# Where the high word of a weight decode is held while the main loop runs

## The chip, the cores and the metric

One core of a Trainium2 chip runs the whole program. The metric is the device time of one execution in microseconds (us), given as the median over runs. The kernel before takes 1439.48 us (three runs, 1436.52 to 1439.56).

## The reference, cut to what matters

The program computes an attention whose keys and values are first packed to 32 rows per head, then a gated layer, then a second layer with two products of x:

```python
p_packed = sm_attn(p, k, v)                 # 8 batches, 8 heads, 32 packed rows, 64 wide
x = sm_attn(q, p_packed, p_packed)          # 576 rows a batch -> 4608 x 512
h = x @ w_in                                # 512 x 2048
x = (h * sigmoid(h)) @ w_out                # 2048 x 512
a = x @ w1; b = x @ w2                      # 512 x 1024 each
out = ((a * b) @ w3) @ wo2                  # 1024 x 1024, 1024 x 512
```

The weights reach the chip as 64-bit words and have to be turned into 32-bit floats there. That is the work this change touches.

## The kernel before, in words

**Decode.** A weight tile of 128 x 512 is loaded as 64-bit words (`raw`). `Decode` (L167) makes floats of it in five instructions. ScalarE scales the high word (L179, shown in the profile under the helper's line L82) and shifts the low word. VectorE shifts the high word into place (L183, `z` or `zi`), and then joins the high word's sign with the low word (L185, written to `raw`). GpSimd adds the two (L189). The scaled high word goes either back into `raw` itself, which lies in SBUF, or into a PSUM tile `ps_dec`; the argument `ps` says which. A tile of w_out is then split into a high part on ScalarE and a low part on GpSimd (`wo<-z`, line L91).

**Which tiles.** `fill` (L701) holds the first 32 decodes in this order: eight tiles of w_in, w_out tiles 0 to 7, eight more of w_in, w_out tiles 8 to 15. A plan written by hand (`START`, L70) says where each is called (`F`) and loaded (`L`), beside the attention's own steps (`P0`, `S0`, ...), the products of packed rows and w_in (`T`, `D`) and stores (`W`). Whoever calls `acc_bank(1, ...)` (L158) gets one of two of the four PSUM banks that later hold the sums of the second product. `bank` (L163) gives one of two banks with the tag `f`, which scores (`ps_s`), transposes (`ps_t`), attention sums (`ps_o`), packed rows (`ps_pk`) and the products of w_in (`ps_m`) share.

**The main loop.** Each item is one batch, half and 128 columns of the hidden layer. `emit_h` makes `ps_h` with 6 matmuls; `emit_g` makes `sg` on ScalarE, `gg` on VectorE (L846), `gh` on ScalarE and `gl` on GpSimd; three items later `emit_x2` adds gh and gl times a w_out tile to four banks `ps_x` with 12 matmuls. There are 2 banks of `ps_h`, 4 buffers of `gg` and 4 each of `gh` and `gl`. So PE can run ahead with `ps_h`, but only by as many items as these buffers hold. Items 0 to 31 use w_out tiles 0 to 7, four rounds of them; items 32 to 39 are the first that use tiles 8 to 15. Between the items stand the packs (`Pack`, L359) of later batches, each with scores, a softmax and a transpose, from item 26 on.

**What sets the order.** The code is written item by item, and a scheduler then orders the instructions of every engine by a simulated time and hands out the buffers; each engine works through its own list strictly in order. `acc` is filled when `emit_x2` is first called, in item 3. From then on, `if acc` is true while the code is written.

Of the kernel before, what the change touches and what calls it, by code (L numbers as in the profile page):

```python
# [23 lines left out]
def attention_swiglu_chain(  # L24
# [133 lines left out]
    def acc_bank(y, name):  # L158

        turns[y] += 1  # L160
        return ps_acc.tile([128, 512], F32, tag=f"acc{2 * y + turns[y] % 2}", name=name)

    def bank(name):  # L163
        return ps_f.tile([128, 512], F32, tag="f", name=name)
# [76 lines left out]
    def at_room(n):  # L241
        return at.tile([128, 512], I32, tag="z", name="z", bufs=NZ)
# [14 lines left out]
    acc = {}  # L257
# [439 lines left out]
    def finish_fill(n, d):  # L697
# [8 lines left out]
            if kind == "i" else w_out[128 * i:128 * i + 128, :] for kind, i in order  # L706
        ],
        finish_fill, fill_raw, lambda n: zi[order[n][1]].bitcast(I32) if order[n][0] == "i" else at_room(n),
        lambda: None if acc else acc_bank(1, "ps_dec"),
    )  # L710


# [688 lines left out]
```

## Time and profile before

| what | value |
|---|---|
| median of three runs | 1439.48 us |
| the profiled execution's own time | 1437.96 us |
| its span | 1436.1 us |
| PE busy in the span | 1390.7 us (97%) |
| DVE, ACT, POOL busy | 901.6, 672.2, 605.5 us |

PE is TensorE, PEld its weight load, DVE VectorE, ACT ScalarE, POOL GpSimd. The average hides stages: PE is busy nearly everywhere, except in roughly the first 180 us, in which the 32 decodes run. So that stretch is looked at by itself.

### The profile page before, as it was taken

How to read it: one execution, taken by the hardware profiler on the slowest of the kernel's cores; microseconds unless marked ns; L12 is line 12 of the kernel's file. 1: busy time of each engine (PE TensorE's matmuls, PEld its weight loads, DVE VectorE, ACT ScalarE, POOL GpSimd, SP SyncE). 2: the span in 40 equal slices, each digit the busy share in tenths (PEclk: the TensorE clock that was granted, in tenths of full speed). 3: DMA queues.
4: the chain of work that ended last, by engine and by line, in shares of the span. 5: the costliest groups of instructions: out<-in, count | busy, mean ns of one | idle time of the engine just before them, and what ended most of it. 6: DMA issues, size and time to landing. Idle time of an engine off the chain costs nothing.

```text
span 1436.1 us, 25890 instructions
## 1 busy us (share of the span) xinstructions
PE 1390.7 (97%) x9548; PEld 1308.4 (91%) x9548; DVE 901.6 (63%) x1687; ACT 672.2 (47%) x1474; POOL 605.5 (42%) x626
## 2 busy tenths in 40 slices
PE   7799899999999999999999999999999999999998
PEld 5578899899999999999998998999999999999998
DVE  5897756558766488666578855635454553645453
ACT  6866556655666555664556544323232231322221
POOL 2778755856779657687567534100000000000000
PEclk9999899999999999999999999999999999999999
DMA  8697544844568343563557667011010110101000
GB/s 319 198 308 253 163 150 142 265 152 146 170 184 249 123 155 121 170 190 116 178 162 252 204 228 298 23 38 46 15 60 1 60 29 31 59 2 60 1 30 30
DMA packets 135967, 193.07 MB, mean 134 GB/s; under 512 B 14496, under 2 KB 92576, under 8 KB 135328
## 3 DMA queue, kind: packets, MB, share of 16 engines
q1 hardware_dynamic: 125344, 178.82, 39.1%
q10 hardware_dynamic: 10496, 12.59, 2.5%
q8 instruction: 75, 1.23, 0.4%
q14 instruction: 52, 0.43, 0.1%
HBM read 132.38 MB, written 58.98 MB: 133 GB/s over the span
## 4 chain that ended last, share of the span: by engine, by line
PE 70%; DVE 9%; DMA 7%; issue 4%; POOL 4%; ACT 4%; SPq 2%; ACTq 0%; DVEq 0%; POOLq 0%
PE ps_ab L1236 24%; PE ps_x L100 6%; PE ps_x L98 6%; PE ps_x L99 6%; PE ps_o L98 5%; PE ps_o L99 5%; PE ps_o L100 5%; PE ps_h L98 3%; PE ps_h L100 3%; PE ps_h L99 3%; SPq L115 2%; DMA mr<-m_d 1%; DMA m_d<-ms 1%; POOL z L189 1%; DVE sbd L251 1%
## 5 line engine op out<-in xcount | busy, mean ns | idle before, releaser
L98 PE MATMUL ps_x<-gh,wo 128*128 128x288 f32 x1024 | 301.9, 298 | 2.7 <-ACT gh L82 1.2
L99 PE MATMUL ps_x<-gh,wo 128*128 128x288 f32 x1024 | 301.0, 296 | 0.0
L100 PE MATMUL ps_x<-gl,wo 128*128 128x288 f32 x1024 | 289.1, 297 | 1.9 <-POOL gl L91 1.6
L91 POOL TENSOR_TENSOR gl<-gg,gh 128x288 fp32r<-128x288 f32 x256 | 227.9, 893 | 101.5 <-ACT gh L82 82.5
L1236 PE MATMUL ps_ab<-xct,w 128*128 128x256 f32 x1728 | 223.0, 284 | 1.7 <-DVE r L1257 1.4
L1236 PEld LDWEIGHTS ps_ab<-xct,w 128*128 128x128 f32 x1728 | 215.6, 190 | 3.0 <-DVE r L1257 1.6
L98 PEld LDWEIGHTS ps_x<-gh,wo 128*128 128x128 f32 x1024 | 193.0, 189 | 6.1 <-DVE xs L883 2.0
L99 PEld LDWEIGHTS ps_x<-gh,wo 128*128 128x128 f32 x1024 | 193.2, 189 | 2.1 <-issue 1.2
L100 PEld LDWEIGHTS ps_x<-gl,wo 128*128 128x128 f32 x1024 | 188.1, 189 | 4.3 <-POOL gl L91 3.6
L82 ACT ACTIVATE gh<-gg 128x288 fp32r<-128x288 f32 x256 | 112.8, 443 | 165.8 <-DVE gg L846 158.2
L91 POOL TENSOR_TENSOR mq<-mr,mq 128x256 fp32r<-128x256 f32 x168 | 136.7, 814 | 109.0 <-DVE mq L86 54.4
L846 DVE SCALAR_TENSOR_TENSOR gg<-sg,ps_h 128x288 f32<-128x288 f32 x256 | 114.6, 448 | 107.3 <-ACT sg L841 55.3
L1236 PE MATMUL ps_ab<-xcb,w 128*128 128x256 f32 x1296 | 177.5, 283 | 0.7 <-ACT w L82 0.4
L98 PE MATMUL ps_h<-a,mq 128*128 128x288 f32 x512 | 155.9, 305 | 18.0 <-DVE gg L846 13.8
L1236 PEld LDWEIGHTS ps_ab<-xcb,w 128*128 128x128 f32 x1296 | 168.1, 189 | 5.6 <-ACT w L82 0.6
L1257 DVE TENSOR_TENSOR r<-p,ps_ab 128x512 f32<-128x512 f32 x72 | 49.2, 683 | 184.3 <-PE ps_ab L1236 184.1
L99 PE MATMUL ps_h<-a,mq 128*128 128x288 f32 x512 | 152.4, 298 | 0.0
L100 PE MATMUL ps_h<-a,mq 128*128 128x288 f32 x512 | 151.9, 297 | 0.0
L841 ACT ACTIVATE sg<-ps_h 128x288 f32<-128x288 f32 x256 | 103.4, 404 | 82.3 <-PE ps_h L100 48.6
L98 PEld LDWEIGHTS ps_h<-a,mq 128*128 128x128 f32 x512 | 96.7, 189 | 25.9 <-DVE gg L846 19.0
L82 ACT ACTIVATE p<-ps_ab 128x512 f32<-128x512 f32 x72 | 43.1, 598 | 146.2 <-PE ps_ab L1236 139.8
L100 PE MATMUL ps_o<-w,abh 128*128 128x512 f32 x280 | 109.5, 391 | 0.0
(172 smaller groups left out, 2645.3 us busy)
## 6 DMA issues: line engine op xcount, KB each, us to landing
mr<-m_d SPq DMA_DIRECT2D x144, 128.0 KB, 2.6
raw<-in_moe_w_dram SPq DMA_DIRECT2D x32, 512.0 KB, 4.4
wz<-wi_d SPq DMA_DIRECT2D x48, 256.0 KB, 3.8
m_d<-ms SPq DMA_DIRECT2D x96, 128.0 KB, 3.0
x_d<-xs SPq DMA_DIRECT2D x20, 576.0 KB, 3.4
raw<-in_moe_w_out_dram SPq DMA_DIRECT2D x22, 512.0 KB, 4.3
out_dram<-ob SPq DMA_DIRECT2D x36, 256.0 KB, 2.0
vr<-in_v_dram SPq DMA_DIRECT2D x14, 640.0 KB, 4.1
```

The source lines that it names most:

```text
L82: A.activation(out=dst, in_=src, func=ACTF.Copy, scale=mul)
L91: (eng or V).tensor_tensor(out=lo, in0=src, in1=hi.bitcast(F32), op=ALU.subtract)
L98: T.matmul(out=dst, lhsT=wh, rhs=xh, start=start, stop=False)
L99: T.matmul(out=dst, lhsT=wl, rhs=xh, start=False, stop=False)
L100: return T.matmul(out=dst, lhsT=wh, rhs=xl, start=False, stop=stop)
L115: return eng.dma_start(out=out, in_=in_)
L189: G.tensor_tensor(out=z, in0=z, in1=word(I32, 0), op=ALU.add)
L251: (act_copy if plain else V.tensor_copy)(dst[r, 0, :, r], src[r])
L841: ins = A.activation(out=sg, in_=ps, func=ACTF.Tanh, scale=0.5)
L846: ins = V.scalar_tensor_tensor(out=gg, in0=sg, scalar=1.0, in1=ps, op0=ALU.add, op1=ALU.mult)
L1236: T.matmul(out=bank[:, x], lhsT=w[:, wp], rhs=xt[:, kt, xp], start=first and (x, kt, n) == (0, 0, 0), stop=last and (x, kt, n) == (1, 1, 2 ...
L1257: V.tensor_tensor(out=dst, in0=p, in1=q, op=op)
```

## The change

The condition stays, but its first branch now gives a shared bank where it gave nothing. The first 14 decodes, written before `acc` is filled, keep their banks. The other 18 (w_out tiles 6 and 7, w_in tiles 8 to 15, w_out tiles 8 to 15) write their high word to one of the two `f` banks and no longer into `raw`.

```diff
         finish_fill, fill_raw, lambda n: zi[order[n][1]].bitcast(I32) if order[n][0] == "i" else at_room(n),
-        lambda: None if acc else acc_bank(1, "ps_dec"),
+        lambda: bank("ps_dec") if acc else acc_bank(1, "ps_dec"),
     )
```

A bank is held from the write on ScalarE to the second read on VectorE, so the scheduler can place such a decode only where one of the two banks is free, between scores, transposes and products. That moves instructions on all engines. VectorE before, at the last decode (`z_2326` is made of w_out tile 15, `gg` are the items' activations, `mq` a prepared piece of packed w_in):

```order
L846 SCALAR_TENSOR_TENSOR gg_1631<-sg_1629,ps_h_1610 128x288
L86 CAST mq_174<-mr_1607 128x2x128
L883 TENSOR_SCALAR xs_1665<-ps_x2_1415 128x288
L846 SCALAR_TENSOR_TENSOR gg_1673<-sg_1671,ps_h_1646 128x288
L86 CAST mq_174<-mr_1643 128x2x128
L883 TENSOR_SCALAR xs_1665<-ps_x2_1417 128x288
L423 TENSOR_REDUCE mx_1699<-ps_s_1685 128x1
L183 TENSOR_SCALAR z_2326<-raw_2264 128x512
L185 SCALAR_TENSOR_TENSOR raw_2264<-raw_2264 128x512
L423 TENSOR_REDUCE mx_1699<-ps_s_1692 128x1
```

This decode stands behind 27 activations, beside the first pack's scores. VectorE now, from the transposes of the third pack (`e`) through the decodes of w_out tiles 13 and 14 (`z_2214`, `z_2271`):

```order
L91 TENSOR_TENSOR e_2195<-ps_t_2196,e_2194 128x384
L91 TENSOR_TENSOR e_2195<-ps_t_2200,e_2194 96x256
L846 SCALAR_TENSOR_TENSOR gg_2637<-sg_2635,ps_h_2616 128x288
L86 CAST mq_174<-mr_2613 128x2x128
L183 TENSOR_SCALAR z_2214<-ps_dec_2215 128x512
L185 SCALAR_TENSOR_TENSOR raw_2119<-ps_dec_2215,raw_2119 128x512
L846 SCALAR_TENSOR_TENSOR gg_2674<-sg_2672,ps_h_2648 128x288
L86 CAST mq_174<-mr_2645 128x2x128
L183 TENSOR_SCALAR z_2271<-ps_dec_2272 128x512
L185 SCALAR_TENSOR_TENSOR raw_2224<-ps_dec_2272,raw_2224 128x512
L469 STREAM_TRANSPOSE pkT_2327<-pk_2322 128x64
L846 SCALAR_TENSOR_TENSOR gg_2710<-sg_2708,ps_h_2685 128x288
```

These two stand behind 42 and 43 activations, and tile 15's behind 44. The first of the last eight decodes (tile 8) moves from behind 16 activations to behind 30.

GpSimd before, at w_out tiles 10 to 12 (`wo10`, `wo11`, `wo12` are the low parts):

```order
L189 TENSOR_TENSOR z_1966<-z_1966,raw_1869 128x512
L189 TENSOR_TENSOR z_2025<-z_2025,raw_1975 128x512
L91 TENSOR_TENSOR wo10_1972<-z_1966,wo10_1972 128x512
L91 TENSOR_TENSOR gl_1523<-gg_1520,gh_1522 128x288
L91 TENSOR_TENSOR wo11_2031<-z_2025,wo11_2031 128x512
L91 TENSOR_TENSOR gl_1565<-gg_1562,gh_1564 128x288
L225 MEMSET mbd_1905 128x1024
L189 TENSOR_TENSOR z_2095<-z_2095,raw_2034 128x512
L91 TENSOR_TENSOR gl_1602<-gg_1599,gh_1601 128x288
L189 TENSOR_TENSOR z_2199<-z_2199,raw_2104 128x512
L189 TENSOR_TENSOR z_2255<-z_2255,raw_2208 128x512
L91 TENSOR_TENSOR wo12_2101<-z_2095,wo12_2101 128x512
```

GpSimd now, at tiles 13 to 15 (`v` is a split of a pack's values, `wi` one of w_in for the packs' products):

```order
L91 TENSOR_TENSOR v_2340<-vr_2192,v_2339 128x768
L189 TENSOR_TENSOR z_2271<-z_2271,raw_2224 128x512
L91 TENSOR_TENSOR v_2340<-vr_2192,v_2339 96x512
L91 TENSOR_TENSOR wo13_2221<-z_2214,wo13_2221 128x512
L91 TENSOR_TENSOR mq_174<-mr_2682,mq_174 128x2x128
L91 TENSOR_TENSOR wo14_2278<-z_2271,wo14_2278 128x512
L189 TENSOR_TENSOR z_2343<-z_2343,raw_2281 128x512
L91 TENSOR_TENSOR wi_2782<-wz_2780,wi_2782 128x512
L91 TENSOR_TENSOR mq_174<-mr_2718,mq_174 128x2x128
L91 TENSOR_TENSOR wi_2787<-wz_2785,wi_2787 128x512
L91 TENSOR_TENSOR gl_2640<-gg_2637,gh_2639 128x288
L91 TENSOR_TENSOR wo15_2350<-z_2343,wo15_2350 128x512
```

The last w_out tiles no longer alternate with single `gl`; they stand between value splits, `mq` and `wi`, and between `wo10` and the end of `wo15` GpSimd now has 4 adds `z`, 5 low parts `wo`, 2 pairs of `v`, 5 `mq`, 5 `gl` and 2 `wi`. On PE, over the same stretch (from the product with tile 10's low part to that with tile 15's), stand 183 matmuls, among them the `ps_h` of items 39 to 47: PE's list now has `ps_h` of item 46 ahead of the low part of tile 13, whose product belongs to item 37.

## Rows read from the trace of the kernel before

**Rows 1.** Stretches of the decode phase: us, busy by engine, PEclk, DMA share, GB/s
```profile
60.00:80.00 20.00, 16.57 (x98) 13.78 (x98) 18.02 (x29) 12.93 (x28) 18.75 (x16) 1.00 0.98 322
80.00:100.00 20.00, 19.37 (x130) 17.61 (x129) 18.54 (x27) 15.34 (x32) 14.48 (x14) 1.00 0.95 301
100.00:120.00 20.00, 17.38 (x103) 13.82 (x103) 17.45 (x28) 11.01 (x27) 15.68 (x17) 1.00 0.93 302
120.00:140.00 20.00, 20.00 (x144) 19.04 (x144) 13.64 (x18) 15.15 (x32) 17.77 (x17) 1.00 0.79 255
140.00:160.00 20.00, 16.60 (x105) 15.05 (x105) 16.69 (x29) 12.33 (x30) 19.07 (x18) 0.91 0.67 203
160.00:180.00 20.00, 17.31 (x111) 17.08 (x110) 15.31 (x35) 10.05 (x29) 12.57 (x14) 0.83 0.39 113
180.00:200.00 20.00, 20.00 (x156) 20.00 (x155) 11.19 (x35) 10.30 (x26) 8.88 (x10) 1.00 0.41 133
200.00:240.00 40.00, 40.00 (x307) 39.82 (x306) 26.14 (x71) 21.92 (x53) 22.92 (x25) 1.00 0.41 131
```

**Rows 2.** Who PE waited for, 60 to 180 us: total, times, longest
```profile
PE ps_h L98 <- DVE gg L846: 9.8, 9, 3.3
PE ps_x L100 <- POOL gl L91: 1.6, 3, 1.2
```

**Rows 3.** VectorE's decode forms, 0 to 250 us: busy us, mean ns, idle before
```profile
L185 DVE SCALAR_TENSOR_TENSOR raw<-raw 128x512 int32<-128x512 int32 x18 | 21.2, 1175 | 0.0
L183 DVE TENSOR_SCALAR z<-raw 128x512 int32<-128x512 int32 x10 | 8.4, 840 | 4.9 <-ACT raw L82 4.9
L183 DVE TENSOR_SCALAR zi<-raw 128x512 int32<-128x512 int32 x8 | 8.1, 1018 | 0.1
L183 DVE TENSOR_SCALAR zi<-ps_dec 128x512 int32<-128x512 int32 x8 | 5.4, 681 | 4.8 <-ACT ps_dec L82 4.8
L185 DVE SCALAR_TENSOR_TENSOR raw<-ps_dec,raw 128x512 int32<-128x512 int32 x8 | 5.4, 680 | 0.0
```

**Rows 4.** Line L183 over the whole run: ns min/median/max, first and last
```profile
L183 DVE TENSOR_SCALAR z<-raw x30: 386/424/1474, 59.7 to 674.7; 128x512 int32<-128x512 int32 x30
L183 DVE TENSOR_SCALAR z<-ps_dec x26: 673/678/692, 42.4 to 820.3; 128x512 int32<-128x512 int32 x26
```

**Rows 5.** VectorE in order of time: the last decode, and the 44th activation
```profile
145.12 0.99 DVE L183 TENSOR_SCALAR z<-raw 128x512 int32<-128x512 int32 x1
...
201.90 0.46 DVE L846 SCALAR_TENSOR_TENSOR gg<-sg,ps_h 128x288 f32<-128x288 f32 x1
```

**Rows 6.** GpSimd's forms, 60 to 180 us: busy us, mean ns, idle before
```profile
L91 POOL TENSOR_TENSOR gl<-gg,gh 128x288 fp32r<-128x288 f32 x36 | 33.7, 944 | 8.0 <-ACT gh L82 7.7 <-POOL zi L189 0.2
L189 POOL TENSOR_TENSOR z<-z,raw 128x512 int32<-128x512 int32 x11 | 15.8, 1437 | 1.3 <-DVE raw L185 1.3
L91 POOL TENSOR_TENSOR wo<-z,wo 128x512 fp32r<-128x512 f32 x11 | 15.3, 1390 | 0.0
L91 POOL TENSOR_TENSOR mq<-mr,mq 128x256 fp32r<-128x256 f32 x16 | 12.9, 804 | 6.7 <-DVE mq L86 6.1 <-issue 0.3 <-DMA x_d<-xs 0.3
...
L91 POOL TENSOR_TENSOR wi<-wz,wi 128x512 fp32r<-128x512 f32 x3 | 3.9, 1323 | 0.0
L91 POOL TENSOR_TENSOR v<-vr,v 128x768 fp32r<-128x768 f32 x2 | 3.9, 1934 | 0.0
L91 POOL TENSOR_TENSOR v<-vr,v 96x512 fp32r<-96x512 f32 x2 | 2.5, 1272 | 0.0
```

**Rows 7.** VectorE in order of time: from a pack's transpose to the next pack's `e`
```profile
162.09 0.25 DVE L469 STREAM_TRANSPOSE pkT<-pk 128x64 f32<-128x64 f32 x1 [1.94 <-ACT pk L464]
...
179.75 0.88 DVE L91 TENSOR_TENSOR e<-ps_t,e 128x384 fp32r<-128x384 f32 x2 [0.37 <-ACT e L82]
```

**Rows 8.** Line L189, GpSimd's add, over the whole run: ns min/median/max
```profile
L189 POOL TENSOR_TENSOR z<-z,raw x54: 1284/1364/1889, 44.1 to 821.6; 128x512 int32<-128x512 int32 x54
```

## The prediction

> **What bounds the kernel now.** I read the page's busy shares first: PE at 97%. Only where PE is not full can this change give or take time, so the second view is the table of stretches [rows 1]. From 180 us on PE is busy without a gap (20.00 of 20, 40.00 of 40). Between 60 and 180 us it is idle for 3.43 + 0.63 + 2.62 + 0 + 3.40 + 2.69 = 12.8 us, and in 140 to 180 us its granted clock averages 0.91 and 0.83, so a part of those two stretches ran at 1.2 GHz instead of 2.4, behind the idle times in them. In the same rows VectorE is at 87 to 93% from 60 to 120 us, GpSimd at 72 to 95% until 160 us, and the DMA engines at 0.93 to 0.98 until 120 us. The third view, who PE waited for [rows 2], names VectorE: 9.8 us in nine waits for the activation `gg`, against 1.6 us for `gl` of GpSimd. The activation itself is short; it comes late because VectorE has other work ahead of it, decodes among it. So VectorE's queue sets the pace up to about 180 us, and PE after it.
>
> **Part 1, the decode on VectorE gets cheaper.** 18 decodes change form. In place they cost VectorE 8.4 + 8.1 us for L183 and 21.2 us for L185, 37.7 us together; from PSUM the same two lines take 0.681 and 0.680 us [rows 3], 18 x 1.361 = 24.5 us. That frees 13.2 us of VectorE. ScalarE's and GpSimd's instructions keep their count.
>
> In place the shift of L183 took from 386 to 1474 ns, out of PSUM from 673 to 692 [rows 4]: the SBUF form is the quicker one when nothing disturbs it. The Trainium skill says why under "Why PSUM operands drop a tier" (VectorE: DVE Perf Modes): a 32-bit operand in PSUM is read at the plain rate, since the fast mode needs both SBUF read ports. By that rule alone the change would lose 18 x (678 - 386) = 5.3 us of VectorE on L183; the means of 840 and 1018 ns in this stretch [rows 3] say that here the undisturbed form is rare, so the sum goes by the means.
>
> **Part 2, the order moves.** A decode now needs one of two banks for which scores, transposes, attention sums and products of w_in also queue. The order shows what follows: the first eight of the 18 shift by a few activations, and the last eight (w_out tiles 8 to 15) from behind 16 to 27 activations to behind 30 to 44. Up to item 30 VectorE and GpSimd therefore lose these eight decodes altogether: on GpSimd alone 8 x (1.437 + 1.390) = 22.6 us [rows 6]. After it they get them back, all at once, and among three packs.
>
> *The early stretch gains.* What can come back is the idle time of PE in 60 to 120 us (6.7 us) and in 140 to 160 us (3.4 us) [rows 1], 10.1 us at most. I take half, 5 us: most of the waits were VectorE's [rows 2], but the DMA queues are full until 120 us [rows 1], and nothing in the change brings w_in and w_out to the core earlier. Bounds: 2 us (DMA keeps the rest) and 9 us.
>
> *The late stretch loses.* The first product with tile 15 belongs to item 39 and stands behind that item's own `gg`, three items on. Before, tile 15 was shifted at 145.12 us, and the 44th activation ran at 201.90 us [rows 5]: it was 57 us early. Now it stands behind 44 activations, thus not early at all, and PE has to wait for a chain: L183 and L185, GpSimd's add, the high part, the low part. How long follows from GpSimd's queue between `wo10` and the end of `wo15`. It holds 4 `z` (5.75 us), 5 `wo` (6.95), 2 pairs of `v` (2 x 3.206 = 6.41), 5 `mq` (4.02), 5 `gl` (4.72) and 2 `wi` (2.65) by the means of [rows 6], 30.5 us in all. PE's 183 matmuls of that stretch, at the pace of the undisturbed rows (40.00 us for 307, 130 ns each [rows 1]), are 23.8 us. PE is in order and needs the last item of that queue, so it stands idle for 30.5 - 23.8 = 6.7 us, if GpSimd never pauses.
>
> It does pause, by VectorE. Between the decodes of tiles 12 and 13 VectorE's list has a transpose of packed rows, their copies, two reductions, three splits and a pack's `e`; the same run of work took from 162.09 to 180.63 us before [rows 7], 18.5 us, of which some 2.4 us were waits, so I take 16 us, and 17.4 us with the decode of tile 13 behind it. GpSimd starts the add of tile 12 about 4.3 us late (behind a pair of `v` and the adds and the low part before it), and between the adds of tiles 12 and 13 it has 1.44 + 2 `mq` + 4 `gl` + 2 `wo` = 9.6 us. The pause is 17.4 - 4.3 - 9.6 = 3.5 us. Together 6.7 + 3.5 = 10.2 us. I take 9.5, somewhat under it, since the copies in that run were unusually slow in the one pack that the rows show. Bounds: 4 us (GpSimd's instructions all near their shortest, no pause) and 15 us (the clock falls to 1.2 GHz in the gaps, as in 160 to 180 us before).
>
> Line L189 took 1284 ns at its shortest against the mean of 1437 [rows 8]. By the Trainium skill (SBUF — State Buffer, "Who interferes with whom") a VectorE instruction with one SBUF input outside the fast modes leaves GpSimd alone, so the decodes would no longer lengthen GpSimd's work; its adds and low parts at 1.29 us each would give 29.4 us for the queue and 1.1 us less for the forecast. No row says how much of the lengthening came from decodes, so this is left out of the sum.
>
> That this stretch has cover is excluded by the rows: PE had no idle time after 180 us, so every wait there is new. What remains after the last decode is PE's work at full pace, as before.
>
> **The sum.** -5 + 9.5 = +4.5 us. On the profiled execution's own 1437.96 us (span 1436.1 and 1.9 around it) that is 1442.5; this execution lies 1.5 us under the median, so the forecast is 1439.48 + 4.5 = 1444.0 us. What a measurement of this kernel can tell from no change is about 0.2%, 2.9 us.
>
> **The rivals.**
> - *The relief wins (faster).* If VectorE was the whole cause up to 180 us, the early gain is its bound of 9 us. And if GpSimd, relieved until item 30, arrives at the late stretch with nothing behind it, the loss is its low bound of 4 us or a little less. Then 1439.5 - 9 + 3.5 = 1434 us. For it: nine of PE's waits were for `gg` [rows 2]. Against it: the DMA share, and an order in which `ps_h` of item 46 is placed ahead of tile 13's product. Chance 0.27.
> - *They cancel.* Gain 7, loss 7, or nothing of either: 1439.5 us. Chance 0.18.
> - *The banks stall PE directly (slower by more).* PE's products of w_in, one bank each, now wait for a decode that holds it through ScalarE's write, ScalarE's second instruction and two VectorE instructions, about 2.7 us. There are 16 of them behind the first items; if every third waits that long, and PE is in order, 14 us are lost on top of a smaller early gain, and the late stretch at 9.5 us: with half of that hidden, 1451 us. For it: the banks are two. Against it: these products also waited for each other's copies before. It decides where VectorE is later than the order supposes. Chance 0.10.
> - *The PSUM form is the slower one.* If the in-place shift were undisturbed in most cases the relief of part 1 would shrink by 5.3 us and the early gain vanish: 1449 us. The means of [rows 3] speak against it; it is counted within the last chance.
>
> The forecast has 0.45. Slower by over 0.2%: 0.45 + 0.10 = 0.55; within 0.2%: 0.18; faster: 0.27. The likeliest case's own range is 1440 to 1450 us (its bounds -9 + 4, +15 - 2, cut where the other cases begin); with a part of the faster and of the bank case the range is 1434 to 1452 us.
>
> **What the profile will show.** Right: L183 and L185 of all 32 decodes at 0.68 us; PE's idle time in 60 to 140 us smaller, its waits for `gg` shorter; then waits of PE for `wo` or `gl` and for `gg` in the stretch of items 37 to 47, some 10 us, where before there was none; GpSimd full there. Wrong: no idle time of PE around items 37 to 47 (then GpSimd or VectorE ran ahead of the pace that I gave them), PE waiting at `ps_m` for VectorE's L185 (the bank rival), or an early stretch with the old idle times (DMA set it). A time under 1436.6 us would make the forecast wrong.

## The result: 1456.2 us, slower by 1.27%, where 1444 was forecast

The changed kernel takes 1456.24 us (median of four runs, 1455.28 to 1458.42) against 1438.62 of the kernel before beside it: ratio 1.0127, 95% interval 1.0109 to 1.0144. The direction was forecast, the size was not: 17.6 us were lost, not 4.5, and the time lies above the range of 1434 to 1452.

### The profile page after: what moved, and what is told of

Read it like the earlier page. It is cut to its first block, busy times and chain, and to the rows that moved or that the text cites. A ratio compares the mean times of both kernels' runs of the same rounds, so it can differ in the third digit from the quotient of the medians.

```text
span 1455.0 us, 25876 instructions
## 1 busy us (share of the span) xinstructions
PE 1396.2 (96%) x9548; PEld 1313.0 (90%) x9548; DVE 892.5 (61%) x1687; ACT 674.9 (46%) x1474; POOL 597.6 (41%) x626
## 4 chain that ended last, share of the span: by engine, by line
PE 72%; DVE 10%; DMA 6%; ACT 5%; issue 3%; SPq 2%; POOL 1%; ACTq 0%; DVEq 0%; POOLq 0%
PE ps_ab L1236 23%; PE ps_x L99 6%; PE ps_x L98 6%; PE ps_x L100 6%; PE ps_o L98 5%; PE ps_o L99 5%; PE ps_o L100 5%; PE ps_h L98 3%; PE ps_h L100 3%; PE ps_h L99 3%; DVE sbd L251 2%; SPq L115 2%; DMA mr<-m_d 1%; DVE gg L846 1%; DMA z<-late_d 1%
## 5 line engine op out<-in xcount | busy, mean ns | idle before, releaser
L91 POOL TENSOR_TENSOR gl<-gg,gh 128x288 fp32r<-128x288 f32 x256 | 223.2, 874 | 114.2 <-ACT gh L82 87.3
L99 PE MATMUL ps_o<-w,abl 128*128 128x512 f32 x280 | 109.6, 391 | 0.0
```

Of the source, the lines that this page charges most:

```text
L91: (eng or V).tensor_tensor(out=lo, in0=src, in1=hi.bitcast(F32), op=ALU.subtract)
L99: T.matmul(out=dst, lhsT=wl, rhs=xh, start=False, stop=False)
```

## The profile after

The stretches of the kernel after, by the columns of [rows 1] (length, busy time of PE, PEld, DVE, ACT and POOL, PEclk, DMA share, GB/s):

```profile
60.00:80.00 20.00, 18.41 (x106) 14.66 (x105) 13.89 (x23) 11.28 (x25) 14.20 (x14) 1.00 0.88 273
80.00:100.00 20.00, 17.66 (x111) 15.34 (x110) 14.08 (x27) 11.35 (x24) 12.97 (x13) 1.00 0.63 216
100.00:120.00 20.00, 15.41 (x88) 11.87 (x86) 12.53 (x22) 10.62 (x22) 9.84 (x11) 1.00 0.75 233
120.00:140.00 20.00, 19.05 (x106) 16.83 (x107) 7.71 (x15) 10.11 (x24) 10.78 (x12) 0.83 0.80 270
140.00:160.00 20.00, 20.00 (x156) 20.00 (x155) 11.79 (x30) 12.72 (x31) 11.04 (x14) 1.00 0.44 153
160.00:180.00 20.00, 17.83 (x124) 17.27 (x123) 13.75 (x36) 13.01 (x33) 12.52 (x13) 0.91 0.31 100
180.00:200.00 20.00, 13.24 (x81) 11.99 (x79) 14.54 (x29) 10.98 (x25) 13.64 (x12) 0.83 0.58 191
200.00:240.00 40.00, 30.15 (x208) 28.64 (x207) 30.07 (x70) 21.71 (x52) 27.38 (x26) 0.91 0.57 175
```

VectorE is relieved, 48.2 us busy from 60 to 140 us where [rows 1] add up to 67.7. But PE is no busier for it, and from 180 to 240 us, where it had no gap before, it is idle for 6.8 + 9.9 = 16.6 us. In those two stretches the granted clock averages 0.83 and 0.91, so parts of them ran at 1.2 GHz: up to 20 x 0.17 + 40 x 0.09 = 7 us more. Who PE waited for, 180 to 242 us (total, times, longest), comes to 16.5 us:

```profile
PE ps_s L98 <- DVE raw L185: 6.3, 1, 6.3
PE ps_h L98 <- DVE mq L86: 3.1, 1, 3.1
PE ps_s L98 <- DVE mbd L492: 1.9, 2, 1.2
PE ps_t L441 <- ACT e L428: 1.3, 1, 1.3
PE ps_pk L478 <- ACT pk L464: 1.1, 1, 1.1
PE ps_o L98 <- DVE e L91: 1.0, 1, 1.0
PE ps_x L98 <- ACT wo L82: 0.8, 1, 0.8
PE ps_x L99 <- POOL wo L91: 0.6, 1, 0.6
PE ps_h L98 <- DVE gg L846: 0.4, 1, 0.4
```

The waits that the forecast named, for `wo` and `gg`, are the small ones (0.8, 0.6 and 0.4). The long one is a pack's scores that wait for a decode to give back a shared bank. ScalarE had written it early, VectorE read it late, as the three engines show in order of time (start, length; in brackets the idle time before):

```profile
210.18 0.61 ACT L82 ACTIVATE ps_dec<-raw 128x512 f32<-128x512 f32 x1
```
```profile
209.72 0.46 DVE L846 SCALAR_TENSOR_TENSOR gg<-sg,ps_h 128x288 f32<-128x288 f32 x1 [0.26 <-ACT sg L841]
210.09 3.68 DVE L251 CAST sbd<-pkT 32x64 fp32r<-32x64 f32 x4
...
214.25 2.44 DVE L253 TENSOR_TENSOR sbd<-pkT,sbd 32x64 fp32r<-32x64 f32 x4
216.72 0.69 DVE L183 TENSOR_SCALAR z<-ps_dec 128x512 int32<-128x512 int32 x1
217.44 0.69 DVE L185 SCALAR_TENSOR_TENSOR raw<-ps_dec,raw 128x512 int32<-128x512 int32 x1
```
```profile
218.19 0.61 PE L98 MATMUL ps_s<-x,pb 128*128 128x288 f32 x1 [6.26 <-DVE raw L185]
```

The last decode holds its bank from 210.18 to 218.13, 8 us, since VectorE's list has the eight block copies of the third pack ahead of it (four casts, L251, and four subtracts, L253, each 32x64). It is the last decode, 72 us later than in [rows 5], behind the 44th activation at 209.72.

GpSimd was not the bound there. What it waited for from 180 to 242 us, and its adds and low parts from 180 to 220 us (busy, mean ns, idle before):

```profile
POOL gl L91 <- ACT gh L82: 9.8, 5, 4.9
POOL mq L91 <- DVE mq L86: 6.0, 5, 2.9
POOL z L189 <- DVE raw L185: 1.9, 1, 1.9
```
```profile
L189 POOL TENSOR_TENSOR z<-z,raw 128x512 int32<-128x512 int32 x6 | 7.8, 1312 | 1.9 <-DVE raw L185 1.9
L91 POOL TENSOR_TENSOR wo<-z,wo 128x512 fp32r<-128x512 f32 x5 | 6.4, 1270 | 0.3 <-ACT wo L82 0.3
```

Its instructions were even shorter than in [rows 6] (1312 and 1270 ns against 1437 and 1390), and in these three lines alone it stood idle for 17.7 us.

*The early stretch.* Between 70 and 94 us SyncE's list issues no load of a w_in tile any more; first it has the stores of four products, whose copies are not there yet (from 65 to 130 us SyncE waited 11.4 us for ScalarE's copies `ms`, 1.4 before). After, then before (SPq is SyncE's queue, L207 the load):

```profile
84.87 6.71 SPq L115 DMA_DIRECT2D m_d<-ms  x4
92.95 0.32 SPq L115 DMA_DIRECT2D x_d<-xs  x1
94.04 1.29 SPq L207 DMA_DIRECT2D raw<-in_moe_w_in_dram  x1
```
```profile
81.56 0.54 SPq L207 DMA_DIRECT2D raw<-in_moe_w_in_dram  x1
```

So the DMA share of 80 to 100 us falls from 0.95 [rows 1] to 0.63, and decodes wait for loads: ScalarE waited 9.0 us for w_in tiles from 65 to 130 us, and not at all before. It then stands with its whole list, the activation's `sg` included:

```profile
118.05 0.65 ACT L82 ACTIVATE raw<-raw 128x512 int32<-128x512 uint32 x1 [2.36 <-DMA raw<-in_moe_w_in_dram]
118.61 0.60 ACT L82 ACTIVATE ps_dec<-raw 128x512 f32<-128x512 f32 x1
119.15 0.39 ACT L82 ACTIVATE xs<-ps_x 128x288 f32<-128x288 f32 x1
119.44 0.70 ACT L841 ACTIVATE sg<-ps_h 128x288 f32<-128x288 f32 x2
```

**PE's lag.** To see where each kernel loses, matmuls are summed in order, each form at one fixed length (the one that a fifth of them stay under in the trace of before), and each trace is asked how much later than before it has done the same amount of work. Columns are moments of before, in us; numbers are us behind it. Single profiles differ by up to 4 us at 80 us without a cause in the kernel (a third buffer in the kernel before, which left its time unchanged, read 4.2 there, with 0.83 granted from 60 to 80 us), so changes along a row count, not its level there.

| bank for | 100 | 120 | 150 | 170 | 180 | 200 | 210 | 250 | 300 | 400 |
|---|---|---|---|---|---|---|---|---|---|---|
| all 18 (after) | 1.1 | 7.0 | 4.5 | -2.9 | -0.9 | 11.3 | 21.4 | 23.1 | 19.2 | 19.3 |
| first ten | 1.5 | 8.1 | 5.8 | 4.6 | 15.2 | 16.3 | 16.5 | 16.5 | 16.9 | 17.3 |
| last eight | 3.3 | 2.8 | 0.0 | -6.9 | -6.4 | 5.9 | 16.1 | 17.8 | 13.8 | 14.3 |
| last eight, called earlier | 3.7 | 3.1 | 0.3 | -7.0 | 0.6 | 5.6 | 5.7 | 5.7 | 6.2 | 6.8 |
| all 18, packs later | 2.9 | 6.4 | 4.0 | 1.2 | -1.1 | 4.0 | 4.2 | 3.4 | 12.6 | 14.5 |
| w_in 8 to 15 | 0.2 | -1.2 | 1.1 | 10.8 | 11.0 | 11.8 | 13.1 | 13.1 | 10.6 | 11.1 |
| w_out 6 and 7 | -0.2 | -0.4 | 0.0 | -2.9 | -1.0 | -1.0 | -0.9 | -0.8 | -1.7 | -1.6 |

In after, PE loses 8.6 us between 110 and 120 us (from -1.6 to 7.0), gets 10 back up to 170, then loses 24 up to 210 and gets 4 back. Of the 8.6, PE's waits for `gg` from 100 to 125 us are 5.1 (0.9 before); the granted clock of 0.83 from 120 to 140 us makes up to 20 x 0.17 = 3.4 more.

## The experiments

The theory at the start was that the last eight decodes make the loss, because they are put late and share two banks with the packs' scores; the rivals were GpSimd's queue, as forecast, and the early decodes. All edits of who gets a bank are in the one line of the change; `fill.n` counts the decodes called.

| run | median us | ratio to before, 95% |
|---|---|---|
| first ten in the bank | 1453.49 | 1.0102, 1.0087 to 1.0118 |
| last eight in the bank | 1453.42 | 1.0106, 1.0090 to 1.0122 |
| all but the last three | 1457.56 | 1.0135, 1.0111 to 1.0158 |
| all 18, packs later | 1451.40 | 1.0086, 1.0064 to 1.0108 |
| w_out 6 and 7 | 1437.29 | 0.9990, 0.9981 to 1.0000 |
| w_in 8 to 15 | 1447.95 | 1.0065, 1.0051 to 1.0078 |
| first ten, called earlier | 1455.12 | 1.0115, 1.0098 to 1.0131 |
| all 18, copies on ScalarE | 1446.96 | 1.0057, 1.0042 to 1.0073 |
| last eight, called earlier | 1443.74 | 1.0035, 1.0024 to 1.0047 |
| all 18, last eight called earlier | 1448.71 | 1.0066, 1.0043 to 1.0090 |
| before, copies on ScalarE | 1434.55 | 0.9970, 0.9958 to 0.9982 |
| w_in 8 to 15, three buffers | 1442.59 | 1.0026, 1.0014 to 1.0038 |
| before, three buffers | 1438.18 | 0.9997, 0.9988 to 1.0007 |
| all 18, three remedies | 1444.07 | 1.0036, 1.0023 to 1.0049 |
| w_out 6 and 7, copies on ScalarE | 1431.18 | 0.9951, 0.9938 to 0.9965 |

### Which half loses

```diff
-        lambda: bank("ps_dec") if acc else acc_bank(1, "ps_dec"),
+        lambda: acc_bank(1, "ps_dec") if not acc else bank("ps_dec") if fill.n <= 24 else None,
```

> The changed kernel with the bank only for the first ten of the 18 decodes (w_out tiles 6 and 7, w_in tiles 8 to 15); the last eight (w_out tiles 8 to 15) go in place as before the change. Theory 1 (the 19 us are lost by the last eight, which are put late in VectorE's order and stand with the packs' scores in two banks, at 180 to 240 us): the late loss goes, 1435 to 1442 us. Rival A (GpSimd's queue, fed late by w_in's decodes as well): a part stays, 1443 to 1450. Rival B (the early decodes are late or hold ScalarE's list at the write into the bank; the trace of after shows w_in's eighth decode 15 us later than before): 1450 or more.

1453.5 us: the first theory failed in this run, and the time is rival B's; the first ten alone lose 14.4 us. By the lag they are 8 us behind at 120 us and lose 10.6 more between 170 and 180, in one stall. In place, w_out tiles 8 to 15 now come 18 to 25 us late (tile 15 is shifted at 168.7 us, not at 145.12 [rows 5]), so GpSimd's work on them runs beside the first pack's copies. VectorE and GpSimd of this kernel, in order of time:

```profile
175.75 4.89 DVE L251 CAST sbd<-pkT 32x64 fp32r<-32x64 f32 x4
180.67 1.28 DVE L86 CAST mq<-mr 128x256 fp32r<-128x256 f32 x1
181.88 5.88 DVE L253 TENSOR_TENSOR sbd<-pkT,sbd 32x64 fp32r<-32x64 f32 x4
187.79 0.22 DVE L490 CAST mbd<-ps_pk 64x64 fp32r<-64x64 f32 x1
188.04 0.46 DVE L846 SCALAR_TENSOR_TENSOR gg<-sg,ps_h 128x288 f32<-128x288 f32 x1
```
```profile
180.50 2.58 POOL L91 TENSOR_TENSOR wi<-wz,wi 128x512 fp32r<-128x512 f32 x2
183.04 0.72 POOL L91 TENSOR_TENSOR mq<-mr,mq 128x256 fp32r<-128x256 f32 x1
183.72 0.78 POOL L91 TENSOR_TENSOR gl<-gg,gh 128x288 fp32r<-128x288 f32 x1
184.47 1.25 POOL L91 TENSOR_TENSOR wo<-z,wo 128x512 fp32r<-128x512 f32 x1
185.69 1.25 POOL L91 TENSOR_TENSOR wi<-wz,wi 128x512 fp32r<-128x512 f32 x1
```

Eight copies of 32x64 take 10.8 us, and the next activation waits behind them (PE 10.1 us at a stretch). Over this kernel such a copy of L253 took from 207 to 5139 ns: the longest ran from 181.88 to 187.02 us, while GpSimd's list ran without a pause until 186.94. The Trainium skill (SBUF — State Buffer, "Who interferes with whom") says that a VectorE instruction with two SBUF inputs, as this subtract is, contends with a GpSimd instruction that reads SBUF, and calls the contention for the shared ports an exclusive lock. These rows agree, and show the wait running on through five of GpSimd's instructions.

```diff
+        lambda: acc_bank(1, "ps_dec") if not acc else bank("ps_dec") if fill.n > 24 else None,
```

> The converse: in place for the first ten of the 18, the bank for the last eight (w_out tiles 8 to 15). Theory 1: the loss stays whole, and without the early relief of VectorE, 1452 to 1460 us. Rival A: 1445 to 1452. Rival B: 1438 to 1442.

1453.4 us, as the theory had it. The lag gains 10 us up to 170 us, since these eight no longer load VectorE and GpSimd early, and loses 23 from 180 to 210. So either half is enough, and the two losses do not add: 14.4 + 14.4 against 17.6 together.

```diff
+        lambda: acc_bank(1, "ps_dec") if not acc else bank("ps_dec") if fill.n <= 29 else None,
```

> The changed kernel with only the last three decodes (w_out tiles 13 to 15) in place: these are the ones that stood latest (204, 206 and 217 us), and the last of them ended the 6.3 us wait of TensorE for a shared bank. If that one wait and what follows it make the loss: 1440 to 1446 us. If the whole list of eight late decodes makes it: 1449 to 1455. If GpSimd's queue makes it, its last items still come in a row: 1448 to 1456.

1457.6 us: no forecast held. The 6.3 us wait for the bank is gone, but the third pack's copies, now from 213.4 to 221.6 us beside GpSimd at 90% busy, take 8.0 us, and PE waits 7.6 us at a stretch for the packed rows' `mbd` (L492) behind them. The wait for a bank was thus not the cause by itself; in these two kernels the row of copies on VectorE held PE by whatever stood behind it.

### Whether place or form

```diff
-    over(26, 38, [Pack(2, 0, 0), Pack(2, 1, 0), Pack(3, 0, 1), Pack(3, 1, 1)])
+    over(32, 44, [Pack(2, 0, 0), Pack(2, 1, 0), Pack(3, 0, 1), Pack(3, 1, 1)])
```

> The changed kernel with the packs 3 and 4 put over items 32 to 44 instead of 26 to 38, all decodes still through the banks: w_out's decodes find room before the scores (places 24 to 36 of VectorE's list, not 30 to 44). If the alternation with the packs' scores in the two banks puts the decodes late and makes the loss: 1438 to 1448 us. If the decodes through a bank cost this whatever their place (ScalarE's list, GpSimd): 1452 to 1460. It has a cost of its own that is not known: the packs' scores then stand later themselves.

1451.4 us, between the two. By the lag the loss of 180 to 210 us is gone (4.2 against 21.4 at 210), but 9 us come at 270 to 300 us, where the packs' own later work is now late.

The cleaner test writes the calls of the last eight earlier and leaves the packs alone:

```diff
-        "| | F L | | F T T | T T | F L | | F L | | F T T | T T | W W | L W W | F L W W | W W "
-        "| F L | F L | F L | F L | F L | F L | F | S0 S1 |"
+        "| | F L | | F T T | T T | F L | | F L | | F L T T | L F L T T | F L W W | F L W W | F L F L W W | F L W W "
+        "| F | F | | | | | | S0 S1 |"
```

> The run with the bank for the last eight decodes alone (w_out tiles 8 to 15; 1453.4 us), and their calls written two to six items earlier, so that most of their banks come ahead of the packs' scores; nothing else moved. By the order they then stand behind 19 to 35 activations, not 30 to 44 (before: 16 to 27). Theory (a bank user waits its turn in the written order, so the decodes are threaded between the steps of the packs, and that place is the whole late loss): 1438 to 1445 us. If decoding through a bank costs this in any place: 1450 to 1456 us.

1443.7 us against 1453.4: two thirds of the late loss were the place, and some 5 us stay. The calls of the loads moved with those of the decodes, but a late load is no rival here: in the run with the old order ScalarE waited for no load from 150 to 222 us. From 200 us on PE is full again, where it was busy for 30.14 of 40 us with the old order:

```profile
200.00:240.00 40.00, 40.00 (x310) 40.00 (x309) 26.35 (x79) 22.51 (x58) 23.51 (x27) 1.00 0.50 159
```

What explains it, by the code and the engines' lists, is the order of the banks. The two go round in the order in which the code asks for them. In place, the scheduler could pull the decode of tile 8, written in item 26, forward to behind the 16th activation. With a bank it must come after all bank users written before it, here the first pack's scores and transposes, and each later one after a step of a pack, which is itself a chain of dependent steps.

The same two lines in the changed kernel:

> The changed kernel, all 18 through the banks, with the calls of the last eight written earlier as in the run before this one. Theory: the loss of 180 to 210 us goes, what w_in tiles 8 to 15 cost early (some 9 us with them alone) stays: 1445 to 1452 us. Rival (early lateness passes on to the last eight wherever they are written, as with the bank for the first ten): 1452 to 1457 us.

1448.7 us, inside the first range: 7.5 us less than the change as it was. The lag at 120 us stays (6.9), that at 210 falls from 21.4 to 9.9.

### Which of the first ten

```diff
+        lambda: acc_bank(1, "ps_dec") if not acc else bank("ps_dec") if fill.n <= 16 else None,
```

> The bank only for the first two of the 18 decodes (w_out tiles 6 and 7); the other sixteen in place. Both keep their places in the order, no product or score is near. Theory now (a decode that must have one of the two shared banks is put behind the products or scores that were written ahead of it, and everything it feeds goes with it): nothing is lost here, 1436 to 1440 us. If the form from PSUM, or the writing of a bank by ScalarE, costs something by itself, eight such decodes less say little, but 1441 or more would speak for it.

1437.3 us, ratio 0.9990: the form from PSUM and ScalarE's write into a bank cost nothing that can be seen where no place is lost (with two decodes, some tenths of a us each could not be seen either).

```diff
+        lambda: acc_bank(1, "ps_dec") if not acc else bank("ps_dec") if 16 < fill.n <= 24 else None,
```

> The bank only for w_in tiles 8 to 15 (eight decodes). In the trace of after the first of them is decoded at 90.9 us, 20 us later than before, and the first load behind it is issued at 94.0 and not at 81.6 us. Theory (early part: these decodes stand behind the products of w_in's first half, which use the same two banks, and the loads of SyncE behind those products' stores): PE loses some 8 us at 110 to 120 us, and w_out's decodes come later: 1446 to 1454 us. If the early decodes are harmless and w_out tiles 6 and 7 with the last eight make the loss: 1437 to 1441 us.

1447.95 us, in the range, but not where it was expected. The lag at 120 us is nil; 10 us are lost between 150 and 170 us. The first of the eight is shifted at 83.7 us (70.9 before), the last w_out tile at 160.6 (145.12), and the first pack's copies beside them take 9.2 us against 6.0 before.

```diff
-        "| F L F L S1 | F L S1 | F F S1 | F F T T | T T | T T | T T L | W W L | F L W W | W W | F L W W | | F L "
-        "| | F L | | F T T | T T | F L | | F L | | F T T | T T | W W | L W W | F L W W | W W "
-        "| F L | F L | F L | F L | F L | F L | F | S0 S1 |"
+        "| F L F L S1 | F L S1 | F F S1 |"
+        " F F L L T T F L F L | T T F L | T T F L | T T F L | W W F L | W W | W W F | W W | | | | | | T T | T T | F | | | | T T | T T | W W "
+        "| L W W | F L W W | W W | F L | F L | F L | F L | F L | F L | F | S0 S1 |"
```

> The run with the bank for the first ten of the 18, and beside it the written order of those ten changed: w_in tiles 8 to 15 are called ahead of or between the products of w_in's first half, so that their banks come first; the last eight in place. By the order the decodes then stand behind 6, 7, 9, 13, 15, 15, 16 and 18 activations, not 11 to 18. If the place in the order makes the early loss: 1438 to 1447 us, against 1453.5 with the bank and the old written order. If the form or the bank itself makes it: 1450 to 1456 us.

1455.1 us, in the range of the second case. Against the run with the old written order the first decodes came 20 us earlier (71.2 and 72.8 us), but the last of the eight was shifted at 125.2 us, as with the old order, and PE lost 13 us between 110 and 120. A late load was not the reason: the eighth tile's was issued at 101.9 us, 11 us earlier than with the old order (113.3). ScalarE wrote this decode's bank at 124.5, behind the copies of two products (123.2 and 124.0). PE meanwhile waited 2.4 us for `mq` and 2.9 us for `a`, the attention's result that the items multiply. So calling these decodes earlier only moved the waiting; that it is their place which costs the early stretch is not shown by this run.

With w_in's eight alone, one more buffer for the products' copies:

```diff
-    NSLOT, LAG, WI, KQ, NZ, NM = 8, 3, 3, 2, 6, 2
+    NSLOT, LAG, WI, KQ, NZ, NM = 8, 3, 3, 2, 6, 3
```

> The run with the bank for w_in tiles 8 to 15 alone (1448.0 us), with three buffers for the products' copies (ms), not two. A product holds a shared bank until ScalarE has copied it, and the copy waits for a buffer whose store has gone. If these stores hold the banks, and with them the decodes and SyncE's loads: 1440 to 1445 us. If not: 1446 to 1450 us.

1442.6 us, 5.4 less than with two buffers. Its control is the same edit in the kernel before:

> The kernel before with three buffers for the products' copies, the control to the run with the bank for w_in tiles 8 to 15 and three buffers (1442.6 against 1448.0 us). If the 5 us were won by freeing banks that decodes wait for: here no change, 1436 to 1440 us. If the third buffer is worth that to any version: 1431 to 1435 us.

1438.2 us, no change. So the third buffer helps only where decodes stand behind products for a bank: more than half of what w_in's eight cost is that. The other 4 us are not accounted for.

### VectorE's list

```diff
-            (act_copy if plain else V.tensor_copy)(dst[r, 0, :, r], src[r])
+            act_copy(dst[r, 0, :, r], src[r])
```

> The changed kernel with the first four of a pack's eight block copies on ScalarE, not VectorE, in all packs. In after the decode of w_out tile 15 stood on VectorE behind the eight copies of the fourth pack, which took 5.9 us, and TensorE waited 6.3 us for the bank that it held. If VectorE's list is what makes the late stretch long: 1446 to 1452 us. If it is the place of the decodes behind the packs whatever VectorE does: 1453 to 1458 us. GpSimd's queue as the bound: no change.

1447.0 us, 9.3 less than the change as it was (the copies ahead of tile 15 are the third pack's, not the fourth's). The control:

> The kernel before, with the first four of a pack's eight block copies on ScalarE as in the run of the changed kernel that came to 1447.0 us. If those 9 us were won by relieving VectorE where the change had crowded it: here 1436 to 1440 us. If the copies are dear everywhere, the 9 us have nothing to do with the change: 1428 to 1434 us.

1434.6 us: 3.9 us are won in the kernel before too (interval of the ratio 0.9958 to 0.9982), which fits neither range whole. So some 5 of the 9 us belong to the change, where VectorE's copies held more behind them.

### Together, and a better version

Three of the edits above in the changed kernel:

> The changed kernel with the three remedies at once: the last eight called earlier, the first four block copies of a pack on ScalarE, three buffers for the products' copies. Singly they gave 7.5 and 9.3 us to the changed kernel, and 5.4 us to the one with w_in's eight alone. If the losses have separate places and add: 1436 to 1441 us. If they overlap, because a later stretch waits anyway for what an earlier one delayed: 1442 to 1448 us.

1444.1 us, so the remedies overlap: 12 us off, where 7.5 + 9.3 alone would be 16.8. The early stretch still loses 6 us at 110 to 120 us, and the whole is 5 us over the kernel before.

The two edits that cost nothing or gained, together:

> The bank for w_out tiles 6 and 7 alone (1437.3 us), with the first four block copies of a pack on ScalarE (1434.6 us on the kernel before). If both small gains are real and add: 1432 to 1435 us. If the bank for two gives nothing: as the kernel before with the copies on ScalarE, 1433 to 1436 us.

1431.2 us, ratio 0.9951 (0.9938 to 0.9965): faster than both kernels, and a little under the expected 1432. That the bank for two adds to the copies' gain is not shown: the interval overlaps that of the copies alone (0.9958 to 0.9982). PE is full from 180 us on as in [rows 1], and the first pack's four copies that stay on VectorE take 5.1 us where eight took 6.0.

## Why the prediction was wrong

*Part 1, the cheaper decode: right.* The forms of the kernel after, 0 to 250 us (busy, mean ns, idle before), against the in-place forms of [rows 3]:

```profile
L183 DVE TENSOR_SCALAR zi<-ps_dec 128x512 int32<-128x512 int32 x16 | 10.9, 682 | 8.0 <-ACT ps_dec L82 8.0
L183 DVE TENSOR_SCALAR z<-ps_dec 128x512 int32<-128x512 int32 x16 | 11.0, 685 | 2.9 <-ACT ps_dec L82 2.6
L185 DVE SCALAR_TENSOR_TENSOR raw<-ps_dec,raw 128x512 int32<-128x512 int32 x26 | 17.6, 678 | 0.0
```

The 0.68 us came as forecast. But VectorE's relief of 19 us from 60 to 140 us left PE no busier there, and the two decodes that keep their places (0.9990, 0.9981 to 1.0000) show little gain from it by itself.

*The early gain of 5 us: the sum came out near by luck, the working did not.* At 170 us PE is 2.9 us ahead. But up to 120 us it had lost, not gained: who PE waited for from 60 to 180 us hardly changed against [rows 2],

```profile
PE ps_h L98 <- DVE gg L846: 8.9, 6, 4.0
PE ps_m L671 <- ACT ms L82: 1.1, 1, 1.1
PE ps_m L671 <- DVE raw L185: 1.0, 1, 1.0
```

and the gain came only at 140 to 170 us, from the eight decodes that were missing there. The working held the DMA queues for a limit that the change leaves alone; in fact it delayed the loads behind the products' stores in SyncE's list. "The first eight of the 18 shift by a few activations" was read as harmless; there are ten of them, and the eight of w_in alone cost 9.6 us.

*The late loss of 9.5 us: the step that failed.* "How long follows from GpSimd's queue": measured are 24 us up to 210 us, 20 net, above the upper bound of 15. The term that was mis-sized is the pause of GpSimd. From the end of `wo10` to the end of `wo15` its queue holds what the prediction counted, but it took 41.6 us and not 34.0:

```profile
184.47 1.29 POOL L91 TENSOR_TENSOR wo<-z,wo 128x512 fp32r<-128x512 f32 x1
...
226.06 1.27 POOL L91 TENSOR_TENSOR wo<-z,wo 128x512 fp32r<-128x512 f32 x1 [0.58 <-ACT wo L82]
```

Its instructions took 27.6 us (30.5 were reckoned) and its pauses 14.1 (3.5 were reckoned). By the prediction's own working, less 23.8 us of matmuls, that makes 17.8 us of idle PE; 16.6 were measured from 180 to 240 us. The clock, which the prediction had in its upper bound alone, makes up to 7 us more. GpSimd waited for ScalarE and VectorE; it was taken for the bound because its list could be added up, and VectorE's run of 16 us between the decodes of tiles 12 and 13 (17.4 with the decode) only for a pause in it. That run came out near what was reckoned: the shifts of tiles 12 and 13 stand at 184.46 and 204.08 us in the trace of after, 19.6 us apart. What the sum left out is what stands behind it: 10.6 us from tile 14 to tile 15 (206.07 and 216.72), through another pack's copies, and PE in order behind each of those steps at packs' scores, `mq` and banks, at a clock that fell as PE paused. "PE had no idle time after 180 us" holds in the kernel before up to 260 us only; from there to 400 us PE was idle for 3.7 us.

*The bank rival had a part of the mechanism, and a chance of 0.10.* PE did wait for a decode to give back a bank, but at a pack's scores and not at the products (`ps_m` for L185: 1.0 us), and for 8 us of holding, not 2.7, since VectorE's list decides when the bank is read. And the dearer part of it is not PE's direct wait: it is the order that the two banks force on the decodes, shown by the runs in which only the calls of the last eight, with their loads, were written earlier (9.7 and 7.5 us).

*GpSimd.* Its add took 1323 ns in the median against 1364 [rows 8], with the same floor (1288 against 1284).

*What stays open.* Which link makes the 8.6 us at 110 to 120 us in the kernels with the first ten in banks: the turn for the bank, the loads behind the products' stores, or ScalarE's list standing at a late load. For the longest wait, 4.0 us up to 120.9, the last link is seen above (`gg` behind `sg` behind ScalarE's 2.4 us at a load); what made that load late is argued from SyncE's list. Nor is it known why the bank for w_out 6 and 7, which costs nothing alone, adds 5.5 us to that for w_in's eight (1453.5 against 1448.0). The third buffer was tried with w_in's eight alone, where the loss falls later, and in the three remedies, which kept this one. It was not shown by itself either how much the copies' length, and how much their place, adds in each stall.

## What to carry to other kernels

A buffer that is shared with a dependent chain costs its place in line, not its bandwidth: before tying early, independent work to such a buffer, look at who asks for it ahead in the written order, and move the calls ahead of that chain. Add up the list of every engine through which the late chain passes, and take as the bound the one in which the row of work behind the chain is longest, not the one that is easiest to add. When a change should relieve an engine, first do it for the few instructions that keep their place: here two of 18 cost nothing that could be seen, and with the copies moved that version beats both kernels, mostly by the copies.

## What the runs showed of the hardware

A copy of 32x64 on VectorE took 175 to 2066 ns in the kernel before, and the subtract beside it up to 5139 ns in another, where its quickest is 207. The size is the same each time; what differs is GpSimd. In the trace of the kernel before, 24 of the 48 casts and 8 of the 48 subtracts took over 330 ns. During these, GpSimd was at work for 99% and 89% of the time on average, and each of the 32 ended 44 to 118 ns after the end of one of GpSimd's instructions. During the shorter ones GpSimd was at work for 7% and 5% of the time. So how long such a small VectorE instruction with SBUF on both sides takes goes by the run of GpSimd's instructions beside it, one or several of them. Before (L251), and with the first ten in banks (L253; min/median/max):

```profile
L251 DVE CAST sbd<-pkT x48: 175/306/2066, 163.0 to 588.4; 32x64 fp32r<-32x64 f32 x48
```
```profile
L253 DVE TENSOR_TENSOR sbd<-pkT,sbd x48: 207/217/5139, 181.9 to 607.3; 32x64 fp32r<-32x64 f32 x48
```
